# Attention's last product in two column tiles, four more pairs turned on TensorE, and a new order from the planner

## The chip, the cores and the metric

The kernel runs on one core of a Trainium2 chip, in one launch. The metric is the device time of that launch in microseconds (us). TensorE (PE in the rows) multiplies, VectorE (DVE) and ScalarE (ACT) work element by element, GpSimd (POOL) does the same for part of the work, and SyncE (SP) issues the DMAs.

## The reference

Random-feature attention over 8 batches of 8 heads, 576 tokens of 64 numbers each, and behind it a feed-forward layer over all 4608 tokens:

```python
    q_s, k_s = (q * scale, k * scale)
    def phi(x):
        proj = np.einsum('bhsd,md->bhsm', x, omega)        # 128 features
        sq = np.sum(x * x, axis=-1, keepdims=True) / 2.0
        h = proj - sq
        h = h - np.max(h, axis=-1, keepdims=True)
        return np.exp(h) / np.sqrt(m)
    q_p, k_p = (phi(q_s), phi(k_s))
    kv = np.einsum('bhsm,bhsd->bhmd', k_p, v)
    z = np.sum(k_p, axis=2)
    num = np.einsum('bhsm,bhmd->bhsd', q_p, kv)
    den = np.einsum('bhsm,bhm->bhs', q_p, z)[..., None] + 1e-06
    ...
    x = attn_out.transpose(0, 2, 1, 3).reshape(4608, 512)  # (num / den)
    h = x @ w_in                                           # 512 -> 2048
    g = h * erf(softplus(h))
    return g @ w_out                                       # 2048 -> 512
```

## The kernel before

**The work.** Attention goes by pairs of heads, 32 in all (`n` from 0 to 31; `2_1` in a name is batch 2, pair 1, so n = 9). The feed-forward layer goes by six groups of tokens (two of 2 x 288 columns, four of 2 x 432); its operands are split into a high part and a rest, so that each of its products is three single-pass matmuls, and the later groups use a seven-product scheme whose sums and differences VectorE and GpSimd make.

**One pair.** The projections of q and k are followed by a maximum (VectorE, `mx`) and an exponential (ScalarE, `fk`, `fq`). `kvp` is the product of k's features with v, with a column of ones for z: it is written in two column tiles, 128 rows by 64 columns of the array each. VectorE or ScalarE copies it to `kh`. The last product `nd` multiplies `kh` with q's features, laid out feature by feature (`qh`): before, one matmul per head and per half of the tokens gives 128 rows, 64 of numerators and 64 of denominators. ScalarE then takes the logarithm of the denominators head by head (`rc<-nd`, 64 rows each), one exponential for both (`rc<-rc`), and VectorE multiplies head by head (`xs<-nd,rc`, 64 rows).

**Two ways of projecting and of turning q.** The first pairs (`n < ROWS`, 8 before) load q and k apart; their squares ride along in the projection (`ppk`, `ppq`, 18 matmuls of 128 rows), and TensorE turns q's features by nine transposes (`pt`), which are copied to `qh`. All later pairs load q and k together (`x`) and once more token by token (`y`, squared and summed to `s`); their projections are narrow ones in two row tiles (`pm`, `p0k`, `p0q`, `p1k`, `p1q`), VectorE flips q's features in blocks of 32 (STREAM_TRANSPOSE), and two DMAs through DRAM (`dq`, `qh<-dq`) put them in place.

**What sets the order.** A planner (`Plan.order`) writes down all operations with a cost per engine, gives each a due time, and runs a list schedule: each engine takes the ready operation that is due first. What comes out is the fixed order of every engine's queue; on the chip an engine waits in that order. The planner adds a price where TensorE goes from one array shape to another (`SWITCH`, `mode` 0, 1, 2: whole, row tiles, column tiles), and one where VectorE and GpSimd want SBUF at once (`port`). PSUM banks for attention are taken in the order in which the operations are written down (`att`, at most five at a time).

```python
COST = dict(mm=0.132, proj=0.222, half=0.2135, tr=0.109, kv=0.97, table=1.3)
SWITCH = ((0.0, 0.12, 0.1), (0.29, 0.0, 0.25), (0.27, 0.25, 0.0))
...
        if n - 1 in BEHIND:
            attend(n - 1, 0.75)
        key_values(n, 0.28)
...
ROWS = 8
BEHIND = range(8, 31)
```

Nearly all instructions are recorded on one line (L1071 before), so the names of the tiles tell them apart.

Of the kernel before, what the change touches and what calls it, by code (L numbers as in the profile page):

```python
# [19 lines left out]
P = 128  # L20
# [48 lines left out]
def blocked(b, q):  # L69
# [14 lines left out]
PIECES = dict(gate=2, rest=2, sqk=2, sqq=2, xrest=2)  # L84

SHARED = ("wshift", "wsign", "wtail", "wrest", "wwhole", "wsum", "xsum", "xhigh", "xrest", "gate",
          "high", "rest")
# [19 lines left out]
class Plan:  # L107
# [44 lines left out]
    def order(self, slots, caps):  # L152
# [28 lines left out]
        port, piece, late, mode = 0.0, 1.0, 0.0, 0  # L181
# [32 lines left out]
        while True:  # L214
            progress = True
            while progress:
                progress = False
                for e in engines:
# [3 lines left out]
                    while ready[e]:  # L222
# [68 lines left out]
            while True:  # L291
                if kind == "idle":
                    idle[x] = True
                elif kind == "done":
# [27 lines left out]
def whole_(n):  # L322

    return n < WHOLE or WHOLE2[0] <= n < WHOLE2[1]


JITTER = ((254.7, 264.7, 4, 378), (505, 555, 0.5, 916), (644.9, 744.9, 1, 989), (809.3, 829.3, 4, 232),
# [19 lines left out]
WHOLE = 32  # L347
WHOLE2 = (0, 0)
LESS = []
ROWS = 8  # L350
# [4 lines left out]
START0 = 51.0  # L355
# [8 lines left out]
TAIL = [("V", 0.69, -1e9)]  # L364
# [11 lines left out]
def build(emit):  # L376
# [111 lines left out]
    def make_sums(key, t0, t1):  # L488
# [9 lines left out]
        for x, y, sign, keys, to in (  # L498
# [4 lines left out]
            pl.op("wsum", [("V", 0.37, -1e9), ("G", 0.75, 3.0)],  # L503
# [61 lines left out]
    def load_both(n):  # L565
# [36 lines left out]
    def project_both(n, t0):  # L602
# [15 lines left out]
        for z, qk in enumerate("kq"):  # L618
# [16 lines left out]
    def flip(n, t0):  # L635
# [4 lines left out]
        pl.op("flip", [("V", 1.3, -1e9)], lambda e: E.flip(f), reads=keys, writes=keys,  # L640
# [4 lines left out]
        qh = a["qh"] = a["ql"] = pl.tile("qh", "qh" + a["nm"], [P, S2])  # L645
# [4 lines left out]
    def key_values(n, t0):  # L650
# [3 lines left out]
        pl.op("kv", [("T", COST["kv"], -1e9)], lambda e: E.key_values(kvp, f, v),  # L654
              reads=[(f, i) for i in range(NC)] + [(v, 0)], writes=[(kvp, 0)], plan=pair_time(n, t0), mode=2)
        whole = whole_(n)
        kh = a["kh"] = pl.tile("kh", "kh" + a["nm"], [P, 2, P], F32 if whole else F32R)
        kl = a["kl"] = kh if whole else pl.tile("kl", "kl" + a["nm"], [P, 2, P], F32R)
        pl.op("kvhigh", [("V", 0.5, -1e9), ("A", 0.6, -1e9)], lambda e: E.kv_high(e, kh, kvp),
              reads=[(kvp, 0)], writes=[(kh, 0)])  # L660
        if not whole:
            pl.op("kvrest", [("V", 0.6, -1e9)], lambda e: E.kv_rest(kl, kvp, kh),
                  reads=[(kvp, 0), (kh, 0)], writes=[(kl, 0)])

    def turn(n, t0):
        a = pairs[n]
        whole = whole_(n)
        lent = ("g", "qh0", 2) if n < NP else ("qh", "qh", None)
        qh = a["qh"] = pl.tile(lent[0], "qh" + a["nm"], [P, S2], F32 if whole else F32R, *lent[1:])
        ql = a["ql"] = qh if whole else pl.tile("ql", "ql" + a["nm"], [P, S2], F32R)  # L670
        for i in range(3):
# [3 lines left out]
            pl.op("turnhigh", [("A", 0.5, -1e9), ("V", 0.5, -1e9)],  # L675
                  lambda e, i=i, pt=pt: E.turn_high(e, qh, pt, i), reads=[(pt, 0)], writes=[(qh, i)])
            if not whole:
                pl.op("turnrest", [("V", 0.56, -1e9)], lambda e, i=i, pt=pt: E.turn_rest(ql, qh, pt, i),
                      reads=[(pt, 0), (qh, i)], writes=[(ql, i)])

    def attend(n, t0):
        a = pairs[n]
# [65 lines left out]
    def attention(n):  # L748
# [705 lines left out]
```

## Time and profile before

| | |
|---|---|
| median of 3 runs | 1011.44 us (1009.12 to 1015.74) |
| the profiled execution | 1016.14 us, span of its instructions 1014.4 us |
| granted TensorE clock, mean | 0.985 of full speed |
| TensorE busy | 978.3 us, 96% of the span |
| VectorE, ScalarE, GpSimd busy | 805.2 us (79%), 675.9 us (67%), 653.9 us (64%) |
| DMA moved | 262.59 MB |

All durations below are of the profiled execution, whose span is 1014.4 us; another 1.7 us of its 1016.14 us lie outside the span. Busy time of TensorE counts a matmul until its end, and matmuls overlap, so the distance from one start to the next is what it really takes.

### The profile page before, as it was taken

The numbers are of one execution on the slowest core, as the hardware profiler recorded it, in microseconds if no ns is written. First come the engines' busy times: TensorE is split into PE (matmuls) and PEld (weight loads), VectorE is DVE, ScalarE is ACT, GpSimd is POOL, SyncE is SP. The second block draws the span as 40 slices with busy tenths as digits, with TensorE's granted clock in tenths as the row PEclk, the third lists the DMA queues.
The fourth block names the chain that finished last, engine by engine and source line by source line (L and its number), as shares of the span: only waits on it lengthen the run. The fifth ranks groups of instructions, "written<-read, shape, count | busy, mean of one in ns | idle before, by whom it ended". The sixth has DMA issues, their size and how long they took to land.

```text
span 1014.4 us, 19023 instructions
## 1 busy us (share of the span) xinstructions
PE 978.3 (96%) x6844; PEld 907.9 (90%) x6844; DVE 805.2 (79%) x1222; ACT 675.9 (67%) x1276; POOL 653.9 (64%) x470
## 2 busy tenths in 40 slices
PE   7999989989999999999999899999999999899998
PEld 6899989979998889999899789999899999899997
DVE  4887988987676878778998979789987888778764
ACT  7979877694776955845677375858649656535650
POOL 4436432954565998577996928298975679656540
PEclk9999999989999999999999989999999999999999
DMA  8376777899897799598788968988788677497661
GB/s 233 107 225 228 255 283 274 278 353 355 266 311 250 252 341 342 187 350 286 254 285 284 363 202 260 295 280 264 262 291 261 218 249 230 149 309 231 224 198 71
DMA packets 112733, 262.59 MB, mean 259 GB/s; under 512 B 12672, under 2 KB 25472, under 8 KB 112640
## 3 DMA queue, kind: packets, MB, share of 16 engines
q1 hardware_dynamic: 112480, 261.31, 77.4%
q8 instruction: 55, 0.90, 0.4%
q14 instruction: 38, 0.31, 0.1%
q10 hardware_dynamic: 160, 0.07, 0.0%
HBM read 204.18 MB, written 57.15 MB: 258 GB/s over the span
## 4 chain that ended last, share of the span: by engine, by line
PE 79%; DVE 8%; ACT 4%; DMA 3%; issue 3%; POOL 2%; SPq 1%; ACTq 0%; DVEq 0%
PE hX L1071 14%; PE oX L1071 12%; PE o L1071 11%; PE h L1071 8%; PE hY L1071 7%; PE oY L1071 6%; PE nd L1071 5%; PE hZ L1071 3%; PE kvp L1071 3%; PE oZ L1071 3%; PE p0k L1071 2%; PE p1k L1071 2%; ACT rc L1071 1%; POOL hs L1071 1%; SPq L1071 1%
## 5 line engine op out<-in xcount | busy, mean ns | idle before, releaser
L1071 POOL TENSOR_TENSOR hs<-gs,hs 128x864 f32<-128x864 f32 (+1 forms) x54 | 114.7, 2149 | 130.2 <-ACT gs L1071 126.0
L1071 PE MATMUL o<-gh,w 128*128 128x288 f32 (+1 forms) x704 | 173.3, 325 | 5.5 <-DVE w L1071 2.8
L1071 PE MATMUL hX<-xh,wb 128*128 128x432 f32 x512 | 168.6, 373 | 3.1 <-DVE hs L1071 3.1
L1071 PEld LDWEIGHTS o<-gh,w 128*128 128x128 f32 x704 | 122.9, 192 | 10.9 <-DVE w L1071 3.9
L1071 PE MATMUL h<-xh,w 128*128 128x288 f32 x512 | 118.5, 310 | 5.4 <-ACT w L1071 2.6
L1071 ACT ACTIVATE hs<-hX 128x432 f32<-128x432 f32 x69 | 36.4, 530 | 125.0 <-PE hX L1071 116.5
L1071 PE MATMUL o<-gl,w 128*128 128x288 f32 (+1 forms) x352 | 111.3, 316 | 0.0
L1071 PEld LDWEIGHTS hX<-xh,wb 128*128 128x128 f32 x512 | 97.8, 191 | 10.4 <-DVE hs L1071 3.4
L1071 PE MATMUL oX<-th,wb 128*128 128x432 f32 x312 | 102.5, 372 | 0.1
L1071 PEld LDWEIGHTS h<-xh,w 128*128 128x128 f32 x512 | 86.7, 192 | 8.0 <-ACT w L1071 2.8
L1071 PE MATMUL hX<-xl,wb 128*128 128x432 f32 x256 | 92.9, 363 | 0.0
L1071 ACT ACT_TABLE_LOAD x68 | 87.2, 1283 | 1.9 <-PEq L1445 0.7
L1071 PE MATMUL nd<-qh,kh 128*128 128x288 f32 x256 | 80.1, 417 | 7.2 <-ACT qh L1071 3.4
L1071 PE MATMUL hY<-xh,wb 128*128 128x432 f32 x256 | 84.7, 369 | 0.0
L1071 PE MATMUL h<-xl,w 128*128 128x288 f32 x256 | 76.5, 299 | 0.0
L1071 ACT ACTIVATE rc<-nd,eps 64x288 f32<-64x288 f32 x128 | 63.6, 497 | 15.9 <-PE nd L1071 12.5
L1071 DVE TENSOR_TENSOR xs<-nd,rc 64x288 f32<-64x288 f32 (+1 forms) x160 | 61.8, 392 | 10.8 <-ACT rc L1071 8.1
L1071 POOL TENSOR_TENSOR tl<-gs,th 128x864 fp32r<-128x864 f32 x28 | 61.3, 2211 | 13.6 <-ACT th L1071 9.0
L1071 DVE TENSOR_TENSOR os<-oX,os 128x432 f32<-128x432 f32 x86 | 51.4, 602 | 23.0 <-PE oX L1071 22.6
L1071 ACT ACTIVATE gs<-hs 128x1728 f32<-128x1728 f32 (+1 forms) x48 | 69.0, 1481 | 0.3
L1071 PEld LDWEIGHTS o<-gl,w 128*128 128x128 f32 x352 | 67.6, 192 | 1.6
L1071 ACT ACTIVATE gs<-gs 128x1728 f32<-128x1728 f32 (+1 forms) x48 | 68.8, 1480 | 0.3
(159 smaller groups left out, 2824.6 us busy)
## 6 DMA issues: line engine op xcount, KB each, us to landing
wb<-wdc SPq DMA_DIRECT2D x232, 256.0 KB, 4.7
wb<-wdw SPq DMA_DIRECT2D x174, 256.0 KB, 5.2
w<-wdw SPq DMA_DIRECT2D x44, 512.0 KB, 7.4
st<-w SPq DMA_DIRECT2D x32, 512.0 KB, 6.3
wdw<-w SPq DMA_DIRECT2D x32, 512.0 KB, 5.9
wdc<-c SPq DMA_DIRECT2D x32, 512.0 KB, 6.9
x<-xR SPq DMA_DIRECT2D x24, 576.0 KB, 6.2
y<-xN SPq DMA_DIRECT2D x24, 576.0 KB, 6.7
```

The source lines that it names most:

```text
L1071: return tc.keep_in_program_order(method(*args, **kwargs))
```

## The change

The last product is now four matmul pairs in column tiles: `attend` writes both heads' denominators into one bank (`nz`, head 0 in rows 0 to 63, head 1 in rows 64 to 127) and both heads' numerators into another (`nd`), once per half of the tokens. Logarithm, exponential and multiplication then each take 128 rows at once. The product stands behind the next pair's `kv` in the same array shape, `kv` is written down ahead of it, and the planner prefers to stay in a tiled shape. `ROWS` goes from 8 to 12, so pairs 8 to 11 take the first pairs' path. The price of the shared port is counted for both engines. The due times are shifted by a list of single dates (`DATES`, 86 entries) where there was a list of windows before (`JITTER`, 43 entries), the feed-forward layer starts 3 us earlier in the planner's dates (`START0`), and some costs are a little different.

```diff
-PIECES = dict(gate=2, rest=2, sqk=2, sqq=2, xrest=2)
+PIECES = dict(gate=2, rest=2, sqk=2, sqq=2, xrest=2, gsum=2, square=2)
+PORT = 0.8
...
-        for lo, hi, amp, k in JITTER:
-            for o in ops:
-                if lo <= o.due < hi:
-                    o.due += amp * ((o.id * 7919 + k * 104729 + 17) % 1009 / 504.0 - 1.0)
+        for i, x in DATES:
+            ops[i].due += x
...
-                    while ready[e]:
+                    if e == "T" and mode:
+                        same = [x for x in ready[e] if x[2].mode == mode and x[2].start is None and can(x[2])]
+                        if same:
+                            chosen = min(same)[2]
+                    while ready[e] and chosen is None:
...
-                        dur += max(0.0, until["G"] - now) % piece
+                        if until["G"] > now:
+                            wait = (until["G"] - now) % piece
+                            if until["G"] - now - wait > 1e-6:
+                                until["G"] += PORT * dur
+                                holder.end = until["G"]
+                            dur += wait
                         port = now + dur
                     elif e == "G":
-                        dur += max(0.0, port - now)
                         piece = dur / PIECES.get(o.name, 1) + 1e-6
+                        dur += PORT * max(0.0, port - now)
+                        holder = o
...
-JITTER = ((254.7, 264.7, 4, 378), (505, 555, 0.5, 916), (644.9, 744.9, 1, 989), (809.3, 829.3, 4, 232),
...
+DATES = ((66, -12.6), (107, -4.7), (117, -40.6), (123, -50.8), (134, -3.2), (171, 10.2), (198, 3.5),
...
-ROWS = 8
+ROWS = 12
...
-START0 = 51.0
+START0 = 48.0
...
+    def attend(n, t0, after=()):
         a = pairs[n]
+        kh, qh = a["kh"], a["qh"]
+        date = pair_time(n, t0) if not after else after[0].plan + 0.01
         for t, (c0, w) in enumerate(SPANS):
             rc = pl.tile(f"rc{t}", f"rc{a['nm']}_{t}", [P, w])
...
+            den, num = (pl.tile("ps", f"{x}{a['nm']}_{t}", [P, 512], F32, "att", early(n)) for x in ("nz", "nd"))
...
+            for x, nd in ((1, den), (0, num)):
+                pl.op("nd", [("T", w / 600, -1e9)],
+                      lambda e, x=x, c0=c0, w=w, nd=nd: E.attend(nd, kh, qh, x, c0, w),
+                      reads=[(kh, 0)] + [(qh, i) for i in c], writes=[(nd, 0)],
+                      plan=date + 0.02 * t, after=after, mode=2)
...
+        key_values(n, 0.28)
         if n - 1 in BEHIND:
-            attend(n - 1, 0.75)
-        key_values(n, 0.28)
+            attend(n - 1, 0.75, (pairs[n]["kv"],))
...
+        def attend(self, nd, kh, qh, x, c0, w):
+            for j in range(2):
+                c = j * S + c0
+                pe.matmul(nd.ap[j * D:(j + 1) * D, :w], lhsT=kh.ap[:, x, j], rhs=qh.ap[:, c:c + w],
+                          start=True, stop=True)
+
+        def log_den(self, rc, den, w):
+            act.activation(rc.ap, den.ap[:, :w], AF.Ln, bias=eps)
...
-        def divide(self, x, nd, rc, j, o, c, w):
-            num = rows(j)[0]
-            dve.tensor_mul(x.ap[num, o:o + w], nd.ap[num, c:c + w], rc.ap[num, c:c + w])
+        def divide(self, x, nd, rc, o, c, w):
+            dve.tensor_mul(x.ap[:, o:o + w], nd.ap[:, c:c + w], rc.ap[:, c:c + w])
```

**The last product and kv on TensorE.** TensorE's queue around the kv product of the last pair (7_3, n = 31), before; `oX` and `oY` are matmuls of the feed-forward layer's second product:

```order
L1071 MATMUL nd_7_2_0_1_9478<-qh_7_2_9216,kh_7_2_9175 128x288
L1071 MATMUL oX4_1_0_9408<-th4_1_0_9313,wb201_9366 128x432
L1071 MATMUL oX4_1_0_9408<-tl4_1_0_9351,wb201_9366 128x432
L1071 MATMUL oX4_1_0_9408<-th4_1_0_9313,wb201_9366 128x432
L1071 MATMUL nd_7_2_1_1_9494<-qh_7_2_9216,kh_7_2_9175 128x288
L1071 MATMUL oX4_1_0_9408<-th4_1_0_9313,wb201_9366 128x432
L1071 MATMUL oX4_1_0_9408<-tl4_1_0_9351,wb201_9366 128x432
L1071 MATMUL oX4_1_0_9408<-th4_1_0_9313,wb201_9366 128x432
L1071 MATMUL kvp_7_3_9506<-v_7_3_9163,fk_7_3_9431 64x2x65 x2
L1071 MATMUL kvp_7_3_9506<-v_7_3_9163,fk_7_3_9431 64x65 x16
```

The last two of the pair's four `nd` matmuls stand one by one among the feed-forward layer's matmuls, and kv comes behind them. The same place on TensorE now:

```order
L1063 MATMUL oX4_1_0_9439<-bb4_1_9270,wb199_9371 128x432 x6
L1063 MATMUL oX4_1_1_9453<-bb4_1_9270,wb199_9371 128x432 x6
L1063 MATMUL oY4_1_0_9464<-th4_1_0_9326,wb200_9395 128x432
L1063 MATMUL oY4_1_0_9464<-tl4_1_0_9354,wb200_9395 128x432
L1063 MATMUL oY4_1_0_9464<-th4_1_0_9326,wb200_9395 128x432
L1063 MATMUL kvp_7_3_9474<-v_7_3_9118,fk_7_3_9433 64x2x65 x2
L1063 MATMUL kvp_7_3_9474<-v_7_3_9118,fk_7_3_9433 64x65 x16
L1063 MATMUL nz_7_2_0_9498<-qh_7_2_9199,kh_7_2_9160 64x288 x2
L1063 MATMUL nd_7_2_0_9503<-qh_7_2_9199,kh_7_2_9160 64x288 x2
L1063 MATMUL nz_7_2_1_9507<-qh_7_2_9199,kh_7_2_9160 64x288 x2
L1063 MATMUL nd_7_2_1_9513<-qh_7_2_9199,kh_7_2_9160 64x288 x2
```

The product is eight matmuls of 64 rows in one row behind kv, in kv's array shape. Ahead of the first row shown stand nine `hX` matmuls and then the last projection of pair 7_3 (`p1q_7_3`).

**Pair 9's projections on TensorE.** The first rows of pair 2_1's projections (n = 9) in TensorE's queue, before:

```order
L1071 MATMUL pm_2_1_2316<-wr_71,x_2_1_1709 128x256
L1071 MATMUL p0k_2_1_2321<-wr_71,x_2_1_1709 128x128
L1071 MATMUL p0q_2_1_2322<-wr_71,x_2_1_1709 128x128
L1071 MATMUL p0k_2_1_2321<-wr_71,x_2_1_1709 128x128
L1071 MATMUL p0q_2_1_2322<-wr_71,x_2_1_1709 128x128
```

They are narrow products in row tiles that take turns. Now the second half of the same pair's projections, where q is projected, with `o0` of the feed-forward layer between:

```order
L1063 MATMUL ppq_2_1_0_2401<-wqk_70,uq_2_1_2135 128x128 x3
L1063 MATMUL o0_2_3_0_2393<-gh0_4_1886,w2_1_3_0_28_2158 128x288
L1063 MATMUL o0_2_3_0_2393<-gl0_4_1906,w2_1_3_0_28_2158 128x288
L1063 MATMUL o0_2_3_0_2393<-gh0_4_1886,w2_1_3_0_28_2158 128x288
L1063 MATMUL ppq_2_1_1_2412<-wqk_70,uq_2_1_2135 128x128 x3
L1063 MATMUL o0_2_3_0_2393<-gh0_5_1903,w2_1_3_0_28_2158 128x288
L1063 MATMUL o0_2_3_0_2393<-gl0_5_1949,w2_1_3_0_28_2158 128x288
L1063 MATMUL o0_2_3_0_2393<-gh0_5_1903,w2_1_3_0_28_2158 128x288
L1063 MATMUL ppq_2_1_2_2427<-wqk_70,uq_2_1_2135 128x128 x3
L1063 MATMUL kvp_2_1_2434<-v_2_1_2169,fk_2_1_2380 64x2x65 x2
L1063 MATMUL kvp_2_1_2434<-v_2_1_2169,fk_2_1_2380 64x65 x16
```

The pair's whole projections (`ppk`, `ppq`) have taken the place of the row tiles, and nine transposes (`pt`) of the pair come later.

**VectorE near the start.** VectorE's queue behind the first pair's `kv`, before; `st`, `wt`, `w1` are steps by which a weight block is made ready:

```order
L1071 TENSOR_SCALAR st1_0_0_142<-st1_0_0_142 128x512
L1071 TENSOR_TENSOR xs0_0_0_277<-nd_0_0_0_0_245,rc_0_0_0_259 64x288
L1071 TENSOR_TENSOR xs0_0_0_277<-nd_0_0_1_0_255,rc_0_0_0_259 64x288
L1071 TENSOR_REDUCE mxq_0_1_286<-ppq_0_1_0_266 128x3
L1071 TENSOR_TENSOR xs0_0_1_313<-nd_0_0_0_1_257,rc_0_0_1_275 64x288
L1071 TENSOR_TENSOR xs0_0_1_313<-nd_0_0_1_1_261,rc_0_0_1_275 64x288
L1071 TENSOR_REDUCE mxq_0_1_286<-ppq_0_1_1_271 128x3
```

And now:

```order
L1063 TENSOR_SCALAR st1_0_0_142<-st1_0_0_142 128x512
L1063 SCALAR_TENSOR_TENSOR wt1_0_0_259<-wt1_0_0_259,st1_0_0_142 128x512
L1063 CAST w1_0_0_1_143<-wt1_0_0_259 128x2x256
L1063 TENSOR_TENSOR xs0_0_0_288<-nd_0_0_0_256,rc_0_0_0_264 128x288
L1063 TENSOR_REDUCE mxq_0_1_290<-ppq_0_1_0_273 128x3
L1063 TENSOR_TENSOR xs0_0_1_298<-nd_0_0_1_268,rc_0_0_1_277 128x288
L1063 TENSOR_REDUCE mxq_0_1_290<-ppq_0_1_1_284 128x3
```

Four multiplications of 64 rows have become two of 128, and the first weight block's steps have moved ahead of them.

## Rows read from the trace of the kernel before

**Rows 1.** The page, busy time by engine: us, share of the span, instructions.

```profile
PE 978.3 (96%) x6844; PEld 907.9 (90%) x6844; DVE 805.2 (79%) x1222; ACT 675.9 (67%) x1276; POOL 653.9 (64%) x470
```

**Rows 2.** Windows, four long stretches, last and sum: length, busy by engine, granted clock, DMA.

```profile
871.00:1005.00 134.00, 134.00 (x685) 128.11 (x684) 96.24 (x109) 65.54 (x60) 63.48 (x31) 1.00 0.63 209
sum 617.00, PE 616.92 PEld 576.22 DVE 482.07 ACT 390.61 POOL 401.65; mean PE 154.23 PEld 144.05 DVE 120.52 ACT 97.65 POOL 100.41
```

**Rows 3.** Windows, nine short stretches between them (eight and their sum), and the start.

```profile
142.00:153.00 11.00, 6.89 (x58) 6.00 (x55) 10.03 (x17) 6.70 (x11) 6.47 (x5) 1.00 0.76 257
153.00:157.00 4.00, 3.71 (x17) 3.71 (x17) 3.79 (x10) 0.61 (x3) 0.00 (x0) 0.57 1.03 418
214.00:222.00 8.00, 5.04 (x37) 4.43 (x36) 7.76 (x17) 7.94 (x9) 3.57 (x3) 0.99 1.01 353
222.00:229.00 7.00, 6.09 (x26) 5.40 (x25) 6.69 (x9) 5.56 (x20) 7.00 (x5) 0.53 1.03 361
322.00:345.00 23.00, 18.34 (x157) 16.90 (x156) 17.88 (x31) 20.02 (x42) 18.99 (x17) 0.93 0.86 295
355.00:362.00 7.00, 5.42 (x22) 4.46 (x19) 6.83 (x6) 3.15 (x6) 7.00 (x4) 0.76 0.68 219
...
579.00:591.00 12.00, 8.15 (x35) 7.06 (x34) 8.55 (x11) 2.08 (x7) 6.68 (x6) 0.72 0.75 223
862.00:871.00 9.00, 5.93 (x22) 5.19 (x22) 7.84 (x6) 1.65 (x1) 9.00 (x6) 0.81 0.31 95
sum 84.00, PE 61.44 PEld 54.78 DVE 72.37 ACT 49.18 POOL 61.71; mean PE 6.83 PEld 6.09 DVE 8.04 ACT 5.46 POOL 6.86
...
0.00:50.00 50.00, 42.02 (x385) 37.09 (x386) 33.08 (x72) 42.23 (x124) 22.23 (x28) 0.97 0.63 170
```

**Rows 4.** Waits of TensorE: who waited for whom, total us, times, longest.

```profile
PE h L1071 <- DVE pm L1071: 2.4, 1, 2.4
PE nd L1071 <- DMA qh<-dq: 2.2, 1, 2.2
```

**Rows 5.** Timeline of TensorE around pair 11's kv: start, us until the last end.

```profile
232.97 2.10 PE L1071 MATMUL nd<-qh,kh 128*128 128x288 f32 x8
235.00 1.38 PE L1071 MATMUL kvp<-v,fk 128*64 128x130 f32 x36
236.31 0.40 PE L1071 MATMUL h<-xh,w 128*128 128x288 f32 x1
```

**Rows 6.** Timeline of TensorE, projection of k and turning of q, early pairs.

```profile
10.74 2.30 PE L1071 MATMUL ppk<-wqk,uk 128*128 128x128 f32 x18
12.87 1.15 PE L1071 MATMUL pt<-ident,fq 128*128 128x128 f32 x9
```

**Rows 7.** Timeline of TensorE, row-tiled projections of pair 25.

```profile
611.67 0.27 PE L1071 MATMUL p0k<-wr,x 64*128 64x128 f32 x1
611.67 0.27 PE L1071 MATMUL p0q<-wr,x 64*128 64x128 f32 x1
611.78 0.27 PE L1071 MATMUL p0k<-wr,x 64*128 64x128 f32 x1
```

**Rows 8.** Groups by shape: count, busy us, mean ns, idle before.

```profile
L1071 ACT ACTIVATE rc<-nd,eps 64x288 f32<-64x288 f32 x128 | 63.6, 497 | 15.9 <-PE nd L1071 12.5
L1071 DVE TENSOR_TENSOR xs<-nd,rc 64x288 f32<-64x288 f32 x96 | 43.4, 452 | 9.1 <-ACT rc L1071 7.3
...
L1071 DVE TENSOR_TENSOR os<-o,os 128x288 f32<-128x288 f32 x48 | 21.4, 452 | 14.8 <-PE o L1071 14.7
```

**Rows 9.** Timeline of VectorE, 572 to 586 us: the longest instruction there.

```profile
575.76 7.47 DVE L1071 TENSOR_TENSOR tl<-gs,th 128x1728 fp32r<-128x1728 f32 x1
```

**Rows 10.** Timeline, pair 31: last projection, last k exponentials, kv.

```profile
797.82 0.27 PE L1071 MATMUL p1q<-wr,x 64*128 64x128 f32 x1
...
801.30 1.17 ACT L1071 ACTIVATE fk<-p1k,mx 128x128 f32<-128x128 f32 x4
...
807.22 0.97 PE L1071 MATMUL kvp<-v,fk 128*64 128x130 f32 x22
```

More of the change, by code (lines that the diff above doesn't have):

```diff
@@ L80 @@
 CAPS = dict(st=3, wt=1, ws=1, wp=2, cv=2, att=5, moe1=5, moe2=3, hs=4, gs=2, w=6, wsums=7)
-PIECES = dict(gate=2, rest=2, sqk=2, sqq=2, xrest=2)
+PIECES = dict(gate=2, rest=2, sqk=2, sqq=2, xrest=2, gsum=2, square=2)
+PORT = 0.8
 SHARED = ("wshift", "wsign", "wtail", "wrest", "wwhole", "wsum", "xsum", "xhigh", "xrest", "gate",
-          "high", "rest")
+          "high", "rest", "gsum", "ptail")
 class Tl:
@@ L180, in order @@
         now, table, lock, bw = 0.0, "exp", None, 0.0
-        port, piece, late, mode = 0.0, 1.0, 0.0, 0
+        port, piece, late, holder, mode = 0.0, 1.0, 0.0, None, 0
         count = 0
@@ L291, in order @@
             while True:
-                if kind == "idle":
+                if kind == "idle" and x == "G" and until["G"] > now + 1e-9:
+                    event(until["G"], kind, x)
+                elif kind == "idle":
                     idle[x] = True
+                elif kind == "done" and x.end > now + 1e-9:
+                    event(x.end, kind, x)
                 elif kind == "done":
@@ L363 @@
 VOS = 5
-TAIL = [("V", 0.69, -1e9)]
+TAIL = [("V", 0.43, -1e9)]
 LATE = 52.68
@@ L639, in flip @@
         keys = [(f, k) for k in range(NC)]
-        pl.op("flip", [("V", 1.3, -1e9)], lambda e: E.flip(f), reads=keys, writes=keys,
+        pl.op("flip", [("V", 1.38, -1e9)], lambda e: E.flip(f), reads=keys, writes=keys,
               plan=pair_time(n, t0))
@@ L644, in flip @@
               reads=keys, writes=[(d, 0)], size=P * S2 * 4)
-        qh = a["qh"] = a["ql"] = pl.tile("qh", "qh" + a["nm"], [P, S2])
+        qh = a["qh"] = pl.tile("qh", "qh" + a["nm"], [P, S2])
         for j in range(4):
@@ L653, in key_values @@
         kvp = a["kvp"] = pl.tile("ps", "kvp" + a["nm"], [P, 512], F32, "att", early(n))
-        pl.op("kv", [("T", COST["kv"], -1e9)], lambda e: E.key_values(kvp, f, v),
+        a["kv"] = pl.op("kv", [("T", COST["kv"], -1e9)], lambda e: E.key_values(kvp, f, v),
               reads=[(f, i) for i in range(NC)] + [(v, 0)], writes=[(kvp, 0)], plan=pair_time(n, t0), mode=2)
[L656 to L659, printed above, removed]
+        kh = a["kh"] = pl.tile("kh", "kh" + a["nm"], [P, 2, 2, D])
+        pl.op("kvhigh", [("V", 0.48, -1e9), ("A", 0.44, -1e9)], lambda e: E.kv_out(e, kh, kvp),
               reads=[(kvp, 0)], writes=[(kh, 0)])
-        if not whole:
-            pl.op("kvrest", [("V", 0.6, -1e9)], lambda e: E.kv_rest(kl, kvp, kh),
-                  reads=[(kvp, 0), (kh, 0)], writes=[(kl, 0)])
     def turn(n, t0):
         a = pairs[n]
-        whole = whole_(n)
         lent = ("g", "qh0", 2) if n < NP else ("qh", "qh", None)
-        qh = a["qh"] = pl.tile(lent[0], "qh" + a["nm"], [P, S2], F32 if whole else F32R, *lent[1:])
-        ql = a["ql"] = qh if whole else pl.tile("ql", "ql" + a["nm"], [P, S2], F32R)
+        qh = a["qh"] = pl.tile(lent[0], "qh" + a["nm"], [P, S2], F32, *lent[1:])
         for i in range(3):
@@ L674, in turn @@
                   reads=[(a["fq"], k) for k in THIRDS[i]], writes=[(pt, 0)], plan=pair_time(n, t0 + 0.05 * i))
-            pl.op("turnhigh", [("A", 0.5, -1e9), ("V", 0.5, -1e9)],
+            pl.op("turnhigh", [("A", 0.5, -1e9), ("V", 0.55, -1e9)],
                   lambda e, i=i, pt=pt: E.turn_high(e, qh, pt, i), reads=[(pt, 0)], writes=[(qh, i)])
-            if not whole:
-                pl.op("turnrest", [("V", 0.56, -1e9)], lambda e, i=i, pt=pt: E.turn_rest(ql, qh, pt, i),
-                      reads=[(pt, 0), (qh, i)], writes=[(ql, i)])
@@ new lines, in attend @@
+            den, num = (pl.tile("ps", f"{x}{a['nm']}_{t}", [P, 512], F32, "att", early(n)) for x in ("nz", "nd"))
+            c = [(j * S + x) // 384 for j in range(2) for x in (c0, c0 + w - 1)]
+            c = sorted({x for i in (0, 2) for x in range(c[i], c[i + 1] + 1)}) if n < ROWS else range(4)
+            for x, nd in ((1, den), (0, num)):
[3 more added lines that the diff above has]
+                      plan=date + 0.02 * t, after=after, mode=2)
@@ L774, in attention @@
             turn(n, 0.5)
-            attend(n, 0.75)
+            if n not in BEHIND:
+                attend(n, 0.75)
     gran = {}
@@ L1120, in halves @@
         return (slice(0, n // 2), slice(n // 2, n)) if e == "G" else (slice(0, n),)
-    def rows(j):
-        return (slice(0, D), slice(D, P)) if j == 0 else (slice(D, P), slice(0, D))
     class Emit:
@@ L1273, in key_values, with kv_out @@
                                   start=False, stop=c == NC - 1)
-        def kv_parts(self, kvp, dst):
-            k = dst.ap.rearrange("p j (h d) -> p (j h) d", h=2)
-            s = kvp.ap[:, :2 * P].rearrange("p (j d) -> p j d", j=2)[:, :, :D1]
-            return (k[:, 0:4:3], s[:, :, :D]), (k[:, 1:3], s[:, :, D:].broadcast_to([P, 2, D]))
-        def kv_high(self, e, kh, kvp):
-            for dst, src in self.kv_parts(kvp, kh):
-                copy(e, dst, src)
-        def kv_rest(self, kl, kvp, kh):
-            for (dst, src), (hi, _) in zip(self.kv_parts(kvp, kl), self.kv_parts(kvp, kh)):
-                dve.tensor_sub(dst, src, hi.bitcast(F32))
+        def kv_out(self, e, kh, kvp):
+            k = kvp.ap[:, :2 * P].rearrange("p (j d) -> p j d", j=2)[:, :, :D1]
+            copy(e, kh.ap[:, 0], k[:, :, :D])
+            copy(e, kh.ap[:, 1], k[:, :, D:].broadcast_to([P, 2, D]))
         def turn(self, pt, f, i):
```

64 lines of the change are left out of this document (16 added, 48 removed), and 25 rows, old and new, of tables (DATES, JITTER).

## The prediction

> **What bounds the kernel now.** I read the page first: TensorE is busy 978.3 of 1014.4 us, far ahead of the others [rows 1]. So the question is where its other 36 us lie, and whether its busy time is all needed. The windows answer it. In four long stretches of together 617 us it is busy 616.92 us, and in the last of them at the full clock (2.4 GHz) it starts 685 matmuls in 134 us, one in 0.196 us [rows 2]. A faster VectorE or ScalarE buys nothing there; only fewer or cheaper matmuls do. The loss sits in nine short stretches of together 84 us, with TensorE busy 61.44, that is 22.6 us idle [rows 3]. Behind an idle moment the granted clock falls to the half level (1.2 GHz) for some us, and busy time counts double there: 6.09 us at 0.53 of the clock, from 222 to 229 us, hold 6.09 × 0.47 = 2.9 us too much. The same product over the other rows with a low clock gives 1.6 (153 to 157), 1.3 (322 to 345), 1.3 (355 to 362), 2.3 (579 to 591) and 1.1 (862 to 871), in all 10.5 us. So 33 us are lost in these stretches. The start loses another 8 (42.02 busy of 50), and some 5 are scattered, the end included.
>
> VectorE is busy 72.37 of those 84 us, in six of the eight rows 85% or more, and ScalarE all but 0.06 of the 8 us from 214 on [rows 3]. The list of waits names what ended them: a maximum of VectorE (`pm`, 2.4 us, at 214 to 222), and a product `nd` that waited 2.2 us for q's round through DRAM, between 322 and 345 [rows 4].
>
> **What the change costs on TensorE.** *The product itself.* Before, eight `nd` matmuls took 235.00 − 232.97 = 2.03 us, 0.25 us each [rows 5]. Now there are 16 per pair, with 64 columns of the array each, two tiles at a time. The trace has no `nd` in column tiles, so I bound it. If the two tiles run side by side, 16 matmuls take the time of eight and the price is 0. If one after the other, it is 8 × 0.25 × 32 pairs = 64 us. The nearest row is kv, which is already in column tiles: 36 matmuls in 1.31 us from its start to the next matmul [rows 5]. A matmul of 128 columns is started every 0.11 us [rows 7], so one of 65 takes some 0.057; 32 of these and four of 130 columns would need 2.28 us one after the other and 1.14 side by side. Measured is 1.31, so side by side. The row-tiled projections say the same: `p0k` and `p0q` start together at 611.67 [rows 7]. I take 0. A gain below 0 is excluded, since the same columns go through the same array.
>
> The Trainium skill ("TensorE: Matmul & The Clock Gate", section "Measured speedup vs the span model") has three column tiles at 2.38 times the speed of one. Taken in proportion, two give 1.59: 128 us of products one after the other become 81 where there were 64, 17 us more, and the time below would be about 1022, an estimate from that page. Kv's row shows 2.28/1.31 = 1.74 with the change of shape in it, better than that page's ratio.
>
> *Changes of the array's shape.* What kv takes beyond 1.14, 0.17 us, I put down to changing the shape [rows 5]. In TensorE's order I count 134 changes before and 184 now, since `nd` leaves the whole array's shape and kv's tiles follow other neighbours: 50 × 0.17 = 8.5 us. Where a change is hidden by a running matmul it costs 0.
>
> *Pairs 8 to 11.* Each now has two projections of 18 matmuls at 12.87 − 10.74 = 2.13 us, and nine transposes at 1.15 − 0.27 = 0.88 (the last one's pass taken off) [rows 6, 7]. Gone are 16 row-tiled pairs of starts at 0.11, 1.76 us, and `pm`'s matmuls, four times 0.11 or 0.44. That is 4.26 + 0.88 − 1.76 − 0.44 = 2.9 us for a pair and 11.8 for four. Together the change puts 20.3 us of work on the engine that sets the time.
>
> **What it takes off the others.** ScalarE's 128 logarithms of 64 rows cost 63.6 us, 497 ns each; 64 of 128 rows are left. That more rows cost nothing is shown by VectorE: `os` over 128 rows and `xs` over 64 both take 452 ns at 288 columns [rows 8]. So some 32 us go on ScalarE, and on VectorE half of the 43.4 us of whole-width `xs`, 22 us, with the narrower ones about 30. Pairs 8 to 11 lose their flips on VectorE and the q traffic through DRAM: `y`, `dq` and `qh` move 0.59 MB each (128 × 1152 × 4 bytes), and in 222 to 229 us DMA already ran at 361 GB/s and a share of 1.03 [rows 3], so about 4.9 us of DMA time a pair. None of it counts in the long stretches. It counts where TensorE waits:
>
> - 214 to 229, lost 3.0 + 0.9 idle and 2.9 by the clock, 6.8: the wait is for pair 9's maximum of row tiles, which no longer exists. I take all of it. What is late next is the same pair's whole maximum `mxq`, with three matmuls of `o0` between its parts as cover.
> - 142 to 157, 4.1 + 0.3 idle and 1.6, 6.0: TensorE takes up new weight blocks of the feed-forward layer there, which VectorE and ScalarE make ready; their work on `rc` and `xs` ahead of these is halved, and the order has moved such steps forward. I take 5.
> - 322 to 345, 4.7 idle and 1.3, 5.9: `nd` waits for DMA, and now stands behind the next kv, so its DMA has some 20 us of TensorE's work as cover where it had 13 by the order. I take 4.
> - the other four, 14.3: VectorE and GpSimd hold each other up. At 575.76 `tl<-gs,th` takes 7.47 us, though its neighbours with fewer columns take about 0.6 [rows 9], and TensorE stands without its operands. The new port model puts such operations elsewhere, and VectorE has less to do. I take two thirds, 10, because with a new order other operations meet at the port, and the next `tl` may meet its like.
>
> **The sum.** 20.3 on, 6.8 + 5 + 4 + 10 = 26 off: 1014.4 becomes 1008.7, a change of −5.7. The profiled execution took 1016.14 us, with 1.7 outside the span, 4.7 above the median of the three runs. I apply the change to the median: 1011.44 − 5.7 is about **1005 us**.
>
> **Rivals.**
>
> *Kv comes too early (slower).* In the new order kv and the product stand as a block, and kv waits for the exponentials of k. Behind the last projection of pair 31 there are nine `hX`, twelve `oX` and three `oY` before it: 24 × 0.196 + 0.17 = 4.9 us. Before, 807.22 − 798.09 = 9.1 us lay there. The chain through maximum and exponentials took from 798.09 (797.82 + 0.27) to 801.30 + 1.17 = 802.47, 4.4 us [rows 10]. So 0.5 us is left, and all of the feed-forward matmuls behind it in TensorE's queue wait along with it. It decides if the chain takes over half a us longer in most of the 20 pairs that still flip. At 1 us a pair it costs 20 us and the time is 1025; clock falls behind the waits come on top, and with half of the 26 not won it is 1035 and more. For it: a margin of 0.5 is smaller than the waits in rows 4. Against it: VectorE and ScalarE, which carry the chain, have 30 us less each.
>
> *The column tiles don't run side by side (the change doesn't do what it says).* With the bound of 64 us the time is 1069; with kv's own ratio, 2.28/1.31 = 1.74, the 128 us of products one after the other become 73.6 where there were 64, 9.6 more, and it is 1015. Kv's 1.31 speaks for the second or for no price, since the rest of it may be the change of shape that is counted next to it.
>
> *All waits go (faster).* If all 33 us go and four of the start's 8, since the feed-forward layer is due 3 us earlier and the first weight block is ready ahead of the multiplications, it is 1014.4 + 20.3 − 37 = 997.7, and the time 995. For it: VectorE is 85% busy or more in six of the eight short stretches shown, and its load falls by 30. Against it: with 20 us more of work the shapes change more often, and new waits arise where an order is made anew.
>
> **How the numbers follow.** The forecast (996 to 1014) has a chance of 0.45, the slower rival 0.27, the faster one 0.22, tiles one after the other or in part 0.06. About 1% (10 us) is what a measurement of this kernel tells from no change. Faster by more needs less than 1001: all of the faster rival and a third of the forecast's cases, 0.37. Slower by more, above 1021.5: most of the slower rival and the tiles, 0.27; the rest is 0.36. The range of 990 to 1030 takes in the forecast, nearly all of the faster rival and half of the slower.
>
> **What would show it.** Right: `nz` and `nd` with two starts of 64 rows together and about 0.25 us to the next two; `rc` 64 times at about 0.5 us and `xs` at half the count; at 214 to 229 no wait for `pm`; TensorE's busy time 10 to 20 us above 978.3, corrected for the clock, and its idle time well under 36. Wrong by the slower rival: waits of `kvp` for `fk` of some 1 us in the late pairs, each with a fall of the clock. Wrong by the tiles: 0.25 us between the two heads' starts. The prediction is also wrong if the long stretches, full to 616.92 of 617 before, show gaps, since all terms above assume that they stay full.

## The result, and the profile after

The changed kernel took 998.17 us (median of 4 runs, 996.58 to 998.89), the kernel before 1012.88 us beside it (1009.12 to 1015.74). The ratio is 0.9855 with a 95% interval of 0.9817 to 0.9892, so 1.1% to 1.8% faster. Forecast were 1005 us and a change of −5.7; measured are −14.7 between the medians. Between the two profiled executions the span goes from 1014.4 to 994.8 us, −19.6; the one of before (1016.14 us) was longer than every one of the runs beside it, so some 5 of the 19.6 us belong to that execution and not to the change.

The page, busy time by engine, after, to be held against [rows 1]:

```profile
PE 982.8 (99%) x7144; PEld 892.6 (90%) x7144; DVE 765.3 (77%) x1139; ACT 664.4 (67%) x1230; POOL 634.9 (64%) x453
```

TensorE's idle time falls from 36.1 to 994.8 − 982.8 = 12.0 us. VectorE has 40 us less to do, ScalarE 11.5, though the logarithms alone give back 32. The windows say where the idle time went. The stretches are cut alike in both kernels; columns as in [rows 2]. The kernel before, start, two middle stretches, and the sum of seven:

```profile
0.00:50.00 50.00, 42.02 (x385) 37.09 (x386) 33.08 (x72) 42.23 (x124) 22.23 (x28) 0.97 0.63 170
...
145.00:230.00 85.00, 77.80 (x638) 71.98 (x637) 72.38 (x130) 65.36 (x151) 51.67 (x48) 0.94 0.88 305
230.00:365.00 135.00, 128.76 (x1100) 120.41 (x1099) 99.84 (x163) 93.88 (x200) 90.33 (x78) 0.97 0.85 284
...
sum 1005.00, PE 973.28 PEld 903.37 DVE 803.41 ACT 675.91 POOL 653.94; mean PE 139.04 PEld 129.05 DVE 114.77 ACT 96.56 POOL 93.42
```

The changed kernel:

```profile
0.00:50.00 50.00, 43.24 (x419) 36.91 (x421) 34.65 (x76) 40.34 (x120) 19.29 (x25) 1.00 0.72 212
...
145.00:230.00 85.00, 85.00 (x758) 78.51 (x757) 66.30 (x124) 66.91 (x147) 50.93 (x45) 1.00 0.80 280
230.00:365.00 135.00, 135.00 (x1183) 124.14 (x1182) 102.87 (x163) 90.64 (x204) 92.83 (x85) 1.00 0.87 293
...
sum 985.00, PE 977.26 PEld 887.62 DVE 763.48 ACT 664.43 POOL 634.95; mean PE 139.61 PEld 126.80 DVE 109.07 ACT 94.92 POOL 90.71
```

From 50 us on, TensorE is idle 955 − 931.26 = 23.7 us before and 935 − 934.02 = 1.0 after. The granted clock is 1.00 throughout; before, with a mean of 0.985, some 0.015 × 1014 = 15 us were lost to the half level. So 22.7 + 15 + 1.2 (start) = 39 us went, against the 26 that I forecast. On the medians, where the change is −14.7, the same sum gives 14.7 + 19.5 = 34. TensorE's work grew by 982.8 − (978.3 − 15) = 19.5 us, against 20.3. The difference of 39 and 19.5 is the −19.6 of the span.

The largest sum of waits before is one that [rows 4] does not show, 9.6 us for VectorE's `hs`, the feed-forward layer's sums of products:

```profile
PE p1q L1071 <- DVE hs L1071: 3.8, 1, 3.8
PE hX L1071 <- DVE hs L1071: 3.1, 1, 3.1
PE hZ L1071 <- DVE hs L1071: 2.7, 2, 1.6
```

These are the idle time of the four stretches 355 to 362, 481 to 484, 579 to 591 and 862 to 871. The waits after, the three longest; those in [rows 4] are gone, and 0.4 us are left for `hs`:

```profile
PE ppk L1063 <- ACT uk L1063: 3.8, 1, 3.8
PE nz L1063 <- ACT qh L1063: 1.9, 2, 1.1
PE hX L1063 <- DVE os L1063: 0.5, 1, 0.5
```

TensorE's timeline at pair 31's kv, where [rows 5] had one kind after the other:

```profile
786.51 1.38 PE L1063 MATMUL kvp<-v,fk 128*64 128x130 f32 x36
787.72 0.66 PE L1063 MATMUL nz<-qh,kh 128*64 128x288 f32 x4
788.21 0.66 PE L1063 MATMUL nd<-qh,kh 128*64 128x288 f32 x4
788.69 0.66 PE L1063 MATMUL nz<-qh,kh 128*64 128x288 f32 x4
789.18 0.66 PE L1063 MATMUL nd<-qh,kh 128*64 128x288 f32 x4
789.76 0.47 PE L1063 MATMUL oY<-th,wb 128*128 128x432 f32 x1
```

The product's 16 records (each of its eight matmuls stands twice in the trace) take 789.76 − 787.72 = 2.04 us, where eight records of whole matmuls took 2.03. The two heads' first matmuls start 8 ns apart, and the next two 0.24 us later: the two tiles run side by side. The Trainium skill ("TensorE: Matmul & The Clock Gate", section "Measured speedup vs the span model") has 2.38 for three column tiles; taken in proportion that was an estimate of 17 us more, and the trace does not agree: two tiles give a factor of 2. The logarithm and the multiplication came out as worked out from [rows 8]:

```profile
L1063 ACT ACTIVATE rc<-nz,eps 128x288 f32<-128x288 f32 x64 | 31.9, 507 | 20.5 <-PE nz L1063 20.2
L1063 DVE TENSOR_TENSOR xs<-nd,rc 128x288 f32<-128x288 f32 x48 | 21.2, 448 | 9.4 <-ACT rc L1063 8.4 <-PE nd L1063 0.8
```

### The profile page after: what moved, and what is told of

The parts are those of the page before. It is cut to its first block, busy times and chain, and to the rows that moved or that the text cites. A ratio compares the mean times of both kernels' runs of the same rounds, so it can differ in the third digit from the quotient of the medians.

```text
span 994.8 us, 19463 instructions
## 1 busy us (share of the span) xinstructions
PE 982.8 (99%) x7144; PEld 892.6 (90%) x7144; DVE 765.3 (77%) x1139; ACT 664.4 (67%) x1230; POOL 634.9 (64%) x453
## 4 chain that ended last, share of the span: by engine, by line
PE 95%; DMA 2%; DVE 2%; ACT 1%; issue 0%; SPq 0%; DVEq 0%
PE o L1063 16%; PE hX L1063 15%; PE oX L1063 12%; PE h L1063 10%; PE hY L1063 7%; PE oY L1063 6%; PE kvp L1063 4%; PE hZ L1063 4%; PE nz L1063 3%; PE oZ L1063 3%; PE nd L1063 3%; PE p0k L1063 2%; PE ppq L1063 2%; PE ppk L1063 2%; PE p1k L1063 2%; DMA st<-w 1%
## 5 line engine op out<-in xcount | busy, mean ns | idle before, releaser
L1063 PE MATMUL o<-gh,w 128*128 128x288 f32 (+1 forms) x704 | 166.4, 317 | 0.1
L1063 PE MATMUL hX<-xh,wb 128*128 128x432 f32 x512 | 161.0, 364 | 0.9 <-DVE os L1063 0.5
L1063 POOL TENSOR_TENSOR hs<-gs,hs 128x864 f32<-128x864 f32 (+1 forms) x44 | 99.0, 2274 | 88.2 <-ACT gs L1063 84.2
L1063 ACT ACTIVATE hs<-hX 128x432 f32<-128x432 f32 x77 | 40.8, 531 | 132.9 <-PE hX L1063 132.7
L1063 PE MATMUL oX<-th,wb 128*128 128x432 f32 x312 | 97.4, 363 | 0.0
L1063 POOL TENSOR_TENSOR tl<-gs,th 128x864 fp32r<-128x864 f32 x34 | 78.6, 2334 | 10.0 <-ACT th L1063 8.9
L1063 PE MATMUL hY<-xh,wb 128*128 128x432 f32 x256 | 80.5, 363 | 0.0
L1063 POOL TENSOR_TENSOR y<-y 128x288 f32<-128x288 f32 x58 | 47.3, 843 | 42.8 <-DMA y<-xN 37.2
L1063 PEld LDWEIGHTS oX<-th,wb 128*128 128x128 f32 x312 | 58.6, 188 | 5.6 <-issue 1.8
L1063 POOL TENSOR_TENSOR gl<-hs,gh 128x576 fp32r<-128x576 f32 (+1 forms) x32 | 51.9, 1644 | 16.5 <-ACT gh L1063 14.2
```

The lines of the kernel that those rows point to most:

```text
L1063: return tc.keep_in_program_order(method(*args, **kwargs))
```

## The experiments

Two theories stood at the start. A: the waits went because VectorE and ScalarE have less to do and pairs 8 to 11 no longer go through DRAM. B: they went because the planner's new numbers make an order that fits the chip. Each run is given by its ratio to the kernel before, run on the same chip, with its interval; a difference of ratios times 1013 us is given as us. The changed kernel stands at 0.9855. Where the dates are left out (they are numbered by operation and fit one kernel only), the comparison is with others without dates.

**1. The halves back, order kept.** Every engine's order stays; only `rc` and `xs` are done in two halves.

```diff
-            act.activation(rc.ap, den.ap[:, :w], AF.Ln, bias=eps)
+            for r in (slice(0, D), slice(D, P)):
+                act.activation(rc.ap[r], den.ap[r, :w], AF.Ln, bias=eps[r])
```

(and the multiplication likewise.)

> The changed kernel with the order of every engine kept, but each logarithm and each multiplication behind the last product made in two halves of 64 rows, as before: 64 ScalarE and 80 VectorE instructions more, some 31 us on each of the two engines. Theory A (the waits went because these two engines have less to do): a good part of the lost 20 us comes back, 1005 us or more, with waits of TensorE for VectorE or ScalarE and granted clock under 1.00. Theory B (the waits went because the order fits the chip better, the freed time lies in slack): within 4 us of the changed kernel.

Measured 0.9878 (0.9826 to 0.9931), 2.3 us more, not apart from the changed kernel by the intervals. The engines did get the work back, DVE 797.6 and ACT 698.5 us on its page:

```profile
PE 985.9 (99%) x7144; PEld 892.9 (89%) x7144; DVE 797.6 (80%) x1219; ACT 698.5 (70%) x1294; POOL 640.2 (64%) x453
```

In this order some 33 us on each engine lie almost wholly beside TensorE's work. Against A as far as the halving goes; but the order was planned with the halved costs, and what the planner would make of full costs with column tiles was not run.

**2. One whole matmul for two tiles, order kept.**

```diff
-            for j in range(2):
-                c = j * S + c0
-                pe.matmul(nd.ap[j * D:(j + 1) * D, :w], lhsT=kh.ap[:, x, j], rhs=qh.ap[:, c:c + w],
-                          start=True, stop=True)
+            pe.matmul(nd.ap[:, :w], lhsT=kh.ap[:, x].rearrange("p j d -> p (j d)"),
+                      rhs=qh.ap[:, (1 - x) * S + c0:(1 - x) * S + c0 + w], start=True, stop=True)
```

> The changed kernel with the order kept, but the last product's two column tiles replaced by one matmul over the whole array, both heads' columns against one head's q (it leaves out half of the right products, so the output is another): four matmuls a pair in place of eight, the same columns through the array. It prices column tiles by themselves. If the tiles run side by side and the change of shape is hidden: within 3 us of the changed kernel. If 0.17 us is paid at each change of shape: up to 5 us faster for the changes that go. If tiles run side by side only in part, as by the ratio of 1.59 or 1.74: 10 to 17 us faster.

Measured 0.9758 (0.9692 to 0.9823), 9.8 us less (its interval just touches that of the changed kernel), more than I expected of the shapes, and by the time alone it could be the tiles running only in part side by side. The trace decides. Three of a pair's four products alone among `hX` and `hY`, in the changed kernel:

```profile
554.47 0.36 PE L1063 MATMUL hY<-xh,wb 128*128 128x432 f32 x1
554.76 0.71 PE L1063 MATMUL nz<-qh,kh 128*64 128x288 f32 x4
555.29 0.66 PE L1063 MATMUL nd<-qh,kh 128*64 128x288 f32 x4
555.78 0.66 PE L1063 MATMUL nz<-qh,kh 128*64 128x288 f32 x4
556.36 0.46 PE L1063 MATMUL hX<-xh,wb 128*128 128x432 f32 x1
556.66 0.36 PE L1063 MATMUL hX<-xl,wb 128*128 128x432 f32 x1
```

And with whole matmuls:

```profile
551.80 0.36 PE L1063 MATMUL hY<-xh,wb 128*128 128x432 f32 x1
551.99 0.65 PE L1063 MATMUL nz<-qh,kh 128*128 128x288 f32 x2
552.48 0.65 PE L1063 MATMUL nd<-qh,kh 128*128 128x288 f32 x2
552.96 0.65 PE L1063 MATMUL nz<-qh,kh 128*128 128x288 f32 x2
553.23 0.57 PE L1063 MATMUL hX<-xh,wb 128*128 128x432 f32 x1
553.64 0.36 PE L1063 MATMUL hX<-xl,wb 128*128 128x432 f32 x1
```

From the last `hY` to the second `hX` it is 2.19 us with tiles and 1.84 without. In both the steps inside are some 0.5 us; most of the 0.35 lies at the two ends. So a visit of the tiled shape costs 0.35 us for going in and out, as twice the 0.17 that I had from kv. The changed kernel's trace has 27 such visits that are not joined to a kv, 9.5 us by this one; TensorE is busy 982.8 − 974.4 = 8.4 us less without them, and 10 us less when the 1.7 us that run 2 lost to a lower clock (0.998) are taken off as well. Where the product is joined to kv, the tiles cost nothing: at pair 31 it is 3.56 us from the start of `kvp` to the second `oY` with tiles (786.51 to 790.07) and 3.55 with whole matmuls (781.84 to 785.39).

**3 and 4. Both kernels without their fitted dates.**

```diff
-DATES = ((66, -12.6), (107, -4.7), ...
+DATES = ()
```

> The changed kernel without its list of single dates: same work, same planner, another order. Theory A: the gain stays, 1003 us or less. Theory B: the dates hold it, 1008 us or more, with the short stretches of waits back in other places.

> The kernel before without its list of windows that shift due times: the same undoing of the fitted dates on the other side. Theory A: it stays well behind the changed kernel without dates, by about 10 us or more. Theory B: both kernels without dates are within some 6 us of one another.

The changed kernel without dates is at 0.9910 (0.9879 to 0.9941), the one before without its windows at 1.0106 (1.0063 to 1.0149). The first lies between what the two theories asked, close to A's 1003 us. The dates are worth about 5.6 us in the changed kernel (the intervals just touch) and the windows 10.7 in the kernel before, and without them on both sides the gap is 20 us, larger than with them. So the gain isn't the dates; it is in the product, the pairs or the planner's rules.

**5 and 6. Pairs 8 to 11.** `ROWS` alone, in both kernels without dates.

> The changed kernel without dates and with ROWS at 8, so that pairs 8 to 11 go the way of the later pairs again; to be held against the changed kernel without dates (0.991 of the kernel before). Theory A (pairs 8 to 11 on TensorE end the waits, work of 11.7 us buys more than it costs): idle time and low clock come back between 150 and 260 us, 5 us or more above it. Theory B (what the planner counts, with kv ahead of the product, makes the order good): 5 us or more below it, since 11.7 us of TensorE's work are saved and no wait returns.

> The kernel before without its windows of shifted dates and with ROWS at 12: pairs 8 to 11 changed alone, with the old product, old planner prices; to be held against the kernel before without windows (1.0106). Theory A: 5 us or more faster than that, in spite of 11.7 us more of TensorE's work. Theory B: 5 to 12 us slower, by the work.

With `ROWS` at 8 the changed kernel without dates is at 0.9877 (0.9823 to 0.9930), 3.3 us less, which the intervals don't part from 0.9910; it reaches the bound of neither theory. The kernel before with 12 is at 1.0201 (1.0143 to 1.0260), 9.6 us more than 1.0106, though these intervals touch. So turning four more pairs on TensorE won nothing in either order, and costs near its 11.7 us in one of them. Theory A falls for this part too.

**7 and 8. The port model, out of the changed kernel and into the kernel before.** The second puts these lines into the kernel before without windows, with `PORT`, `PIECES` and `SHARED` as in the change and two conditions that keep the planner's GpSimd busy for the time added; the first takes only the lines shown out again:

```diff
-                        dur += max(0.0, until["G"] - now) % piece
+                        if until["G"] > now:
+                            wait = (until["G"] - now) % piece
+                            if until["G"] - now - wait > 1e-6:
+                                until["G"] += PORT * dur
+                                holder.end = until["G"]
+                            dur += wait
...
-                        dur += max(0.0, port - now)
+                        dur += PORT * max(0.0, port - now)
+                        holder = o
```

> The changed kernel without dates and with the port counted as before (a wait for VectorE of at most one piece, none of it put on GpSimd's time). Theory A: within 5 us of the changed kernel without dates. Theory B: slower by 5 us or more, with waits of TensorE for VectorE's `hs` and `os` of 2 us and more, as before.

> The kernel before without its windows of shifted dates, and with the port counted both ways in the planner: that alone, nothing else of the change. To be held against the kernel before without windows (1.0106 of the kernel before). Theory P (the port model makes the order good, whatever the product): 8 us or more faster, as its removal from the changed kernel without dates cost 9. Theory R (the port model only pays where VectorE has been relieved): within 4 us.

Out of the changed kernel without dates: 1.0000 (0.9968 to 1.0032), 9 us more, and TensorE waits for `hs` 6.0 us again (not for `os`, where I expected it too):

```profile
PE hZ L1045 <- DVE hs L1045: 4.0, 2, 2.4
PE hX L1045 <- DVE hs L1045: 2.0, 1, 2.0
```

Into the kernel before: 0.9898 (0.9835 to 0.9960), 21 us less than 1.0106, with the old product, `ROWS` at 8 and no dates. That is by itself as good as the changed kernel, within the intervals. Its page:

```profile
PE 972.7 (97%) x6844; PEld 899.4 (90%) x6844; DVE 800.7 (80%) x1228; ACT 685.7 (69%) x1276; POOL 640.6 (64%) x465
```

And the waits for `hs`, in run 4 without the new price (L1058) and in run 8 with it (L1069):

```profile
PE hZ L1058 <- DVE hs L1058: 3.7, 1, 3.7
PE hX L1058 <- DVE hs L1058: 2.3, 1, 2.3
PE h L1058 <- DVE hs L1058: 2.2, 1, 2.2
PE hZ L1069 <- DVE hs L1069: 0.4, 1, 0.4
```

From run 4 to run 8 TensorE's idle time falls from 38.4 to 27.4 us, 7.8 of these 11 by the waits for `hs`, and its busy time by 6.8, at a granted clock of 0.996 where it was 0.989. The same waits part all the traces: without the new price they are 9.6 us (the kernel before), 8.2, 12.8 and 6.0 (runs 4, 6 and 7), and with it at most 1.8, in ten traces with seven different orders. So these waits do not hang on the luck of one order, though how much of the 21 us does is not shown. Which operation the price moved, and from where, was not followed.

**9. A delay in front of kv, order kept.** The second four of k's exponentials are made three times in the pairs from 12 on.

> The changed kernel with its order kept, and the second four of k's exponentials of each pair from 12 on made three times (the same values): ScalarE is 2.3 us later with k's features in 20 pairs. It tests the slower rival's point, that kv has only 0.5 us to spare. In the changed kernel's trace the last exponential ends 1.0 to 1.2 us ahead of kv in most of these pairs. If that is the whole cover: waits of kv for ScalarE of some 1.2 us in about 14 pairs, the clock lower, 1012 to 1025 us. If the chain has more slack than the trace shows (ScalarE catches up, other work gives way): within 5 us of the changed kernel.

Measured 0.9958 (0.9929 to 0.9987), 10.4 us more, between the two cases that I had set. The waits of kv in its trace:

```profile
PE kvp L1063 <- ACT fk L1063: 2.5, 4, 0.6
```

Only 2.5 us are waits of kv itself. TensorE's idle time rises from 12.0 to 18.2 us in all: besides the 2.5 for kv, 1.9 are waits of `nz` and `pt` for the exponentials behind the added ones, and 1.7 come at 17 us, before the first delayed pair, with a fall of the clock behind them. Its busy time rises by 5.0, some 2 of it by the clock (0.998); the rest is not settled. The price is at most 0.5 us for each of the 20 pairs, for 2.3 us of delay: the chain has slack, as in the changed kernel's trace, where pair 31's last exponential starts at 784.9, takes 0.43 us and ends 1.2 us ahead of kv at 786.51. I had 0.5 us there, and the rival did not decide.

**10. The old product in the new rules.** One whole matmul per head, both banks kept to the end, logarithm and multiplication in halves, priced double in the planner; `ROWS` 8, no dates, against 0.9877.

> The changed kernel without dates, ROWS at 8, and the last product as before: one whole matmul per head and half of the tokens, logarithm and multiplication by 64 rows. To be held against the changed kernel without dates with ROWS at 8 (0.9877). Theory P (order): the column tiles are only a cost, so it is 5 to 10 us faster by the changes of shape that go, about 0.980. Theory R (relief of VectorE and ScalarE): 31 us more on each of these engines and banks held longer bring waits back, 5 us or more slower.

Measured 1.0156 (1.0080 to 1.0233), 28 us more; the version that by runs 1, 2 and 5 should have been the fastest is the slowest but one. Three waits of TensorE in it:

```profile
PE hX L1051 <- POOL bb L1051: 9.3, 1, 9.3
PE hY L1051 <- ACT fk L1051: 6.3, 1, 6.3
PE hX L1051 <- ACT fk L1051: 3.5, 1, 3.5
```

Behind the longest, 9.3 us for GpSimd's `bb`, stands one VectorE instruction:

```profile
524.87 13.66 DVE L1051 TENSOR_TENSOR hs<-gs,hs 128x1728 f32<-128x1728 f32 x1
```

GpSimd at the same time:

```profile
526.23 4.07 POOL L1051 TENSOR_TENSOR xl<-xc,xh 128x864 fp32r<-128x864 f32 x2
530.24 3.98 POOL L1051 TENSOR_TENSOR hs<-gs,hs 128x864 f32<-128x864 f32 x2
534.16 2.56 POOL L1051 TENSOR_TENSOR y<-y 128x288 f32<-128x288 f32 x4
538.69 0.91 POOL L1051 TENSOR_SCALAR bb<-hs 128x864 fp32r<-128x864 f32 x1 [1.97 <-DVE hs L1051]
```

VectorE ends 1.8 us after the last of an unbroken row of GpSimd's instructions (536.7); the shortest of the same instructions in this trace take 1.9 us, so it looks as if it had not begun before. The three waits come to 19 us beside the 28. The old product does not bring them by itself: run 8 has it too, and TensorE waits there for `fk` 1.4 us at the longest and not for `bb`. Whether the longer hold on the banks or merely another order brought these operations together is not settled.

**11 and 12. Where the product stands, and the planner's single costs.** In run 11 `attend(n - 1, 0.75)` stands ahead of `key_values(n, 0.28)` again, without the preference for a tiled shape; in run 12 eleven of the planner's entries (ten costs and `START0`) have their old values. Both with `ROWS` 8 and no dates, against 0.9877.

> The changed kernel without dates, ROWS at 8, with the product of the pair before written down ahead of kv and at its old date again, not behind kv, and without the preference for a tiled shape: still in column tiles. Against 0.9877. If product and kv as one block matter only by the shapes: 4 to 9 us slower, since each product then stands alone, about 0.36 us for each visit of the tiled shape that is not joined to kv. If kv not waiting for banks matters as well: 10 us or more slower, with waits back.

> The changed kernel without dates, ROWS at 8, with the planner's single costs as before (eleven numbers, among them the start of the feed-forward layer 3 us later). Against 0.9877. If these numbers matter: 5 us or more slower. If they are noise: within 4 us.

Run 11: 1.0058 (1.0019 to 1.0098), 18 us more. Its trace has 51 visits of the tiled shape that are not joined to kv where the changed kernel has 27; 24 more at 0.35 are 8.4 us. The rest is waits and the lower clock behind them (0.991), not of kv for banks, as I had put it, but first of all of the product for q's round through DRAM:

```profile
PE nz L1047 <- DMA qh<-dq: 5.9, 4, 2.6
```

Behind kv that round has the longer cover (the changed kernel waits for it not at all, run 5 neither); this bears out the step for 322 to 345 us. Run 11 undoes the place and the preference for a tiled shape together, and does not say which of the two counts. Run 12: 0.9869 (0.9808 to 0.9929), no difference.

## Why the prediction was right, and where it was off

**The costs on TensorE** were right in sum, 19.5 us against 20.3, and two of the three terms are shown. The product at 0: 2.04 us a pair against 2.03. The shapes at 8.5: 8.4 to 10 in the trace, 9.8 in run 2's time, though they come as visits of 0.35 us that stand apart from kv. The pairs at 11.8 are shown only roughly: the sum leaves 10 to 11, run 6 had 9.6 and run 5 3.3 in time.

**The step that was mis-sized** is the other side, "20.3 on, 26 off": it was 39 between the profiled executions and about 34 on the medians. All nine stretches filled up, not two thirds to five sixths of them. I also counted 10.5 us for the half clock in them by multiplying busy time with what the mean clock lacks. But the low clock falls almost wholly on busy time there: length times what the clock lacks gives 13.4, and 1.5 more at the start, which I had put at nothing, make the 15. The rival "all waits go" came nearest, with 37 and 995 us.

**The cause holds for some of the four terms and not for others.** I put 214 to 229 us (6.8) down to pairs 8 to 11. In runs 4 and 8 these pairs go the old way and that wait for `pm` is not in TensorE's list either, so it belonged to one order; runs 5 and 6 show no gain from the pairs. I gave the halved work of ScalarE and VectorE most of 142 to 157; run 1 puts that work back at a cost of 2.3 us. From 140 to 160 us run 4 waits 4.1 us, run 8 1.7 and run 3 not at all: the port model takes over half of it away with the old product. The 4 us of 322 to 345, for the product behind kv, are borne out by run 11. The 10 us of the last four stretches had the right cause and were too few: their idle time is the 9.6 us of waits for `hs`, which the port model takes away in run 8 and which run 7 brings back. In all it takes 21 us from the kernel before alone, and the changed kernel loses 9 without it. That the time fell within the range is in part luck: 6.8 and most of 5 of the 26 us were put down to what did not win them, and the port model won more than I gave it. What remains of the relief is what run 10 leaves open: the old product in these rules, in that order, is 28 us slower.

**The gain is therefore** mostly that of the port model, with kv ahead of the product as a condition for the tiles (run 11, 18 us) and the dates (5.6). These do not add up to 14.7; each run that is planned anew makes a new order, and parts replace one another. The port model alone reached 0.9898, all of the change without its dates 0.9910. Between these two, run 8 (TensorE busy 972.7 of 1000.1 us, clock 0.996) and run 3 (985.1 of 1003.5, clock 1.000), the rest of the change takes another 12.6 us of idle time and half clock away and puts 16 us of work on TensorE, so column tiles and pairs 8 to 11 use up what they and the new place of the product win.

**The rivals.** Kv too early: not so, slack 1.2 us where I had 0.5, and run 9 prices the miss at no more than 0.5 us a pair for 2.3 us of delay. Tiles one after the other or side by side only in part: excluded by the starts. The other signs came as the prediction has them: `rc` 64 times at 507 ns, `xs` at half the count, no wait for `pm`, and no gap in the long stretches (1.0 us idle from 50 to 985 us).

## What to carry to other kernels

Where one engine is busy 96% and a planner sets the order, ask first whether the planner counts what the other engines do to each other; here that rule (21 us into one kernel, 9 out of the other) was worth more than halving the last product's work on two engines (2.3 us with the order kept). Price a new array shape by visits, about 0.35 us in and out here, and place the work beside something that has the shape already. A change in such an order is read as an order, not as a sum of parts: run the parts alone in both directions before one of them is given the gain.

## What was not expected of the hardware

VectorE can be kept waiting by a whole row of GpSimd's instructions, not just by one. The 13.66 us of run 10 end 1.8 us behind the row; the 7.47 us of [rows 9] end at 583.23, 1.8 us behind GpSimd's row of two-input instructions (to 581.43), in the kernel before:

```profile
579.26 2.17 POOL L1071 TENSOR_TENSOR gs<-hs,gs 128x432 f32<-128x432 f32 x2
581.51 3.22 POOL L1071 TENSOR_SCALAR th<-gs 128x1728 fp32r<-128x1728 f32 x1
```

The Trainium skill ("SBUF — State Buffer", section "SBUF: two separate sides") says that the pair of ports is locked for one instruction and that the loser blocks. These two rows fit that for each instruction, but the loser did not get its turn between two of the winner's. Run 6 has a third, a VectorE cast (`th<-gs`) of 9.34 us that ends 0.9 us behind such a row, ahead of TensorE's longest wait there (5.6 us for `hs`). The planner's price, old and new, has VectorE wait for at most the piece that GpSimd is at, so it is too low in these three places. Longer single instructions did not go away with the change: GpSimd's and VectorE's `tl<-gs,th` take 2334 and 2705 ns on average after, 2211 and 2771 before, and the shortest of VectorE's 1.9 us in both.

```profile
L1063 POOL TENSOR_TENSOR tl<-gs,th 128x864 fp32r<-128x864 f32 x34 | 78.6, 2334 | 10.0 <-ACT th L1063 8.9 <-DVE c L1063 0.6
L1063 DVE TENSOR_TENSOR tl<-gs,th 128x1728 fp32r<-128x1728 f32 x9 | 24.3, 2705 | 0.3 <-ACT th L1063 0.3
```

So for this operation the collisions are still there, and TensorE no longer waits behind them. That the planner moved them to where they do no harm is how I read it; it was not traced operation by operation.
